# An identity load on another queue, a table spread and one product on GpSimd, and a new order of the work

## The chip, the cores and the metric

The kernel runs on one core of a Trainium2 chip. A core has TensorE (PE, matrix products into PSUM), VectorE (DVE), ScalarE (ACT), GpSimd (POOL) and SyncE (SP), which here only issues DMA transfers. Each engine works through its own list of instructions in order; semaphores tie the lists together. The metric is the time of one execution on the device, in microseconds (us). In the profile PEld are TensorE's weight loads, and SPq or ACTq is the issue of a transfer by SyncE or ScalarE.

## What is computed

The sequence length is 2048, the width 448 and the hidden width of the network 1792. A convolution mixer (a short shift filter, then a filter as long as the sequence) is followed by a network over the sequence positions; both have layer norms and residual sums.

```python
def _A_ref(q, k, v, shift_k, ssm_k, ssm_D):
    ...
    for t in range(ks):
        k_shift = k_shift + k_pad[:, t:t + S, :] * shift_k[:, ks - 1 - t][None, None, :]
    kv = k_shift * v
    ...
    y_f = kv_f * kf_f[None, :, :, :]
    y = irfft2(y_f)[:, 0, :S, :].astype(bfloat16)
    y = y + kv * ssm_D[None, None, :]
    return q * y

def _B_ref(x, w1, b1, w2, b2):
    h = _layernorm(x, axis=-1)
    u = jnp.einsum("bsd,sf->bdf", h, w1) + b1
    u = _gelu(u)
    y = jnp.einsum("bdf,fs->bds", u, w2) + b2
    return y.transpose(0, 2, 1)

h = x + _A_ref(_layernorm(x), A_k, A_v, A_shift_k, A_ssm_k, A_ssm_D)      # x = A_q
h2 = h + _B_ref(_layernorm(h), B_w1, B_b1, B_w2, B_b2)
```

## The kernel before

The 2048 positions lie as 128 partitions by 16 rows (r = 0 to 15). The long convolution is done as a Fourier transform in two stages by matmuls, a product, and the inverse in two stages.

The steps have short names, which the order uses:

- con: tables are loaded (L866). con.0 is the identity for the transposes, con.1 the first-stage table E0, con.2 the compact second-stage table FC. con.3 to con.6 spread FC into the table FW, one strided quarter each (L881 on ScalarE, L882 on VectorE), 128x1024 each; all four must be done before the second stage. con.7 to con.12 are tables of the inverse.
- loads: the inputs (L906 ssm_k, four blocks loads.1 to loads.4; L909 and L912 the shift weights, loads.5; L917 k, loads.6, 7, 9 and 11; L920 v; L924 ssm_D; L927 and L929 biases). xload (L934): q in four blocks of four rows, for the layer norm.
- kT: ssm_k is transposed by TensorE with the identity (L1083), eight transposes a step, and copied out of PSUM (L801 or L804). kT.0 and kT.1 are its first block, kT.2 and kT.3 the second, and so on.
- kv: k is transposed in the same way (L986), filtered by matmuls against diagonal weights (L1012, which L971 on GpSimd prepares) and multiplied by v on VectorE (L1051).
- k1 and u1: first transform stage of the filter and of kv, eight small matmuls a step (L1110; L1115 adds ssm_D), then a cast out of PSUM (L1126) on ScalarE or VectorE. Every second step a shuffle, a transfer from on-chip memory to itself (L1130), moves a quarter into the layout of the second stage. k1.0 to k1.7 are half as wide.
- k2 and u2: second stage, eight matmuls with FW (L1150) for two row pairs, and casts out of PSUM (L801/L802 on ScalarE, L804/L805 on VectorE).
- i1: the spectra are multiplied (L1176, 128x1792, VectorE, sixteen products), 64 small matmuls follow for each pair of products (L1195), two casts by ScalarE (L801) and two shuffles (L1210, L1215). zero is a memset on GpSimd (L1161).
- q and xn: statistics of the rows of q (L1252, L1254 on VectorE), then L1260 and the power -0.5 (L1263) on GpSimd, and the normalised rows 0 to 3 (L1285).
- i2: second inverse stage and what follows row by row: matmuls (L1316, L1321), a gate (L1330 on ScalarE, L1332 on VectorE), L1340 or L1351, statistics (L1357, L1360, L1369 and others), the power on GpSimd (L1396) and the normalised row (L1402).
- mlp: the network. Rows 0 to 15 for the first seven column blocks (L1449), the other seven blocks (L1459), the activation (L1439), the second matrix (L1470), the last sum (L1473), the output (L1478 to L1484).
- dummy and warm: matmuls whose result nobody reads (L1071, L1226).

The planner (_Sched) doesn't choose the order: the text ORDER lists for each engine every operation, as step:number, and so names the engine too. Its estimates and landing times (est, late, in nanoseconds) give each operation a modelled time, from which the slots of PSUM and of the small rings are assigned; the instructions and their waits are then written out. The first inverse stage is guarded by a mode: a product on VectorE and one on GpSimd aren't modelled as running together.

An engine goes through its list in order, so an operation that waits holds everything behind it on that engine, and a transfer that waits on SyncE holds the transfers behind it.

## Time and profile before

| | us |
|---|---|
| median of 3 runs | 171.25 |
| lowest, highest | 170.89, 171.83 |
| the profiled execution | 171.0 |
| its span in the profile | 169.2 |
| TensorE busy | 160.5 (95%), 1821 matmuls |
| VectorE busy | 94.5 (56%), 192 instructions |
| ScalarE busy | 88.1 (52%), 133 instructions |
| GpSimd busy | 17.4 (10%), 33 instructions |

The shares of the whole span hide that the stages differ: VectorE and ScalarE are full in the first 90 us and nearly idle afterwards. A busy TensorE isn't TensorE at its peak, since the ends of matmuls are modelled. The rows of the profile name a line of the kernel, an engine, an operation, the output and input with their shapes, the count, the busy time and the mean duration in ns; in a list in order of time the first two numbers are the start and the duration, and the bracket says how long the engine had been idle before, and what ended that. "Time to landing" of a transfer is from its issue to the arrival.

### The profile page before, as it was taken

What the parts mean: (1) busy time and instruction counts of PE and PEld (TensorE: products, weight loads), DVE (VectorE), ACT (ScalarE), POOL (GpSimd) and SP (SyncE); (2) the same over time, 40 slices, a digit from 0 to 9 for tenths busy, and PEclk for the clock granted to TensorE, in tenths of its full rate; (3) what the DMA queues carried; (4) which work ended last, traced back from release to release, by engine and by line L of the source; (5) the groups of instructions that cost most, each with busy time, mean ns of one, the idle gap of its engine ahead of it and who ended that gap; (6) DMA issues with size and microseconds to landing.
All of it is one profiled execution on the core that took longest, in us unless ns stands there. A gap on an engine that the chain in (4) does not pass through costs nothing.

```text
span 169.2 us, 4200 instructions
## 1 busy us (share of the span) xinstructions
PE 160.5 (95%) x1821; PEld 99.8 (59%) x1821; DVE 94.5 (56%) x192; ACT 88.1 (52%) x133; POOL 17.4 (10%) x33
## 2 busy tenths in 40 slices
PE   4999999999988988999999999999999999999994
PEld 1677777433333766644555555555567777777784
DVE  3149889999999999999987710000003223132232
ACT  3389998899999688899777508311210000000000
POOL 1013000000421000054253210000000000000000
PEclk9999999999999999999999999999999999999999
DMA  4999959689939344575899999990000111101111
GB/s 135 344 344 405 412 224 350 244 262 338 414 113 341 125 164 172 219 267 182 288 398 403 410 421 418 417 406 16 0 4 0 54 54 54 54 4 54 54 54 54
DMA packets 16416, 36.69 MB, mean 217 GB/s; under 512 B 2253, under 2 KB 9934, under 8 KB 16398
## 3 DMA queue, kind: packets, MB, share of 16 engines
q1 hardware_dynamic: 16254, 36.34, 57.7%
q8 instruction: 14, 0.23, 0.5%
q10 hardware_dynamic: 144, 0.08, 0.2%
q14 instruction: 4, 0.03, 0.0%
HBM read 23.69 MB, written 1.84 MB: 151 GB/s over the span
## 4 chain that ended last, share of the span: by engine, by line
PE 75%; ACT 14%; DVE 4%; DMA 3%; SPq 1%; issue 1%; POOL 1%
PE ps L1470 25%; PE ps L1449 13%; PE ps L1459 13%; PE ps L1110 6%; ACT arena L801 6%; PE ps L1012 4%; ACT arena L1126 4%; PE ps L1150 4%; PE ps L1195 3%; ACT arena L802 3%; DMA arena<-in_A_ssm_k_dram 3%; PE ps L986 2%; PE ps L1316 2%; DVE arena L1252 2%; PE ps L1083 2%; DVE arena L1176 1%
## 5 line engine op out<-in xcount | busy, mean ns | idle before, releaser
L1473 DVE SCALAR_TENSOR_TENSOR arena<-ps,arena 128x448 bf16<-128x448 f32 (+2 forms) x17 | 11.2, 657 | 57.5 <-PE ps L1470 57.5
L1470 PE MATMUL ps<-arena 128*128 128x448 bf16 (+2 forms) x238 | 42.7, 342 | 0.0
L1470 PEld LDWEIGHTS ps<-arena 128*128 128x128 bf16 x238 | 33.2, 144 | 9.5
L801 ACT CAST arena<-ps 128x896 bf16<-128x896 f32 (+1 forms) x28 | 23.2, 883 | 4.9 <-PE ps L1195 3.8
L1126 ACT CAST arena<-ps 128x896 bf16<-128x896 f32 (+2 forms) x28 | 21.5, 815 | 1.9 <-PE ps L1110 0.9
L1449 PE MATMUL ps<-arena 128*128 128x448 bf16 x112 | 22.4, 353 | 0.0
L1459 PE MATMUL ps<-arena 128*128 128x448 bf16 x112 | 21.4, 352 | 0.0
L1439 ACT ACTIVATE arena<-ps,arena 128x448 bf16<-128x448 f32 x14 | 8.2, 640 | 20.6 <-PE ps L1459 14.7
L1195 PE MATMUL ps<-arena 64*32 64x448 bf16 x512 | 16.1, 350 | 1.3 <-ACT arena L801 1.3
L1449 PEld LDWEIGHTS ps<-arena 128*128 128x128 bf16 x112 | 10.9, 98 | 10.6 <-ACT arena L1330 0.6
L1176 DVE TENSOR_TENSOR arena<-arena 128x1792 bf16<-128x1792 bf16 x16 | 17.0, 1086 | 0.0
L1459 PEld LDWEIGHTS ps<-arena 128*128 128x128 bf16 x112 | 11.0, 98 | 10.2 <-ACT arena L1439 0.2
L1110 PE MATMUL ps<-arena 128*32 128x448 bf16 (+2 forms) x288 | 16.6, 335 | 0.4
L1150 PE MATMUL ps<-arena 128*64 128x448 bf16 x128 | 14.7, 359 | 1.8 <-ACT arena L801 1.2
L1195 PEld LDWEIGHTS ps<-arena 64*32 64x32 f16 x512 | 11.6, 90 | 5.8 <-ACT arena L801 3.2
L1150 PEld LDWEIGHTS ps<-arena 128*64 128x64 f16 x128 | 5.6, 108 | 10.5 <-ACT arena L801 3.3
L1110 PEld LDWEIGHTS ps<-arena 128*32 128x32 f16 x288 | 7.3, 95 | 5.9 <-ACT arena L802 2.1
L804 DVE COPY arena<-ps 128x1024 bf16<-128x1024 bf16 (+1 forms) x9 | 5.7, 658 | 7.8 <-PE ps L1083 7.4
L1051 DVE TENSOR_TENSOR arena<-ps,arena 128x512 bf16<-128x512 f32 (+1 forms) x16 | 9.0, 617 | 1.0 <-PE ps L1012 0.9
L1252 DVE BATCH_NORM_STATS2 arena<-arena 128x6 f32<-128x448 bf16 x16 | 9.4, 607 | 0.0
L805 DVE TENSOR_SCALAR arena<-ps 128x896 bf16<-128x896 f32 x8 | 8.5, 1087 | 0.9 <-PE ps L1150 0.8
L1330 ACT ACTIVATE arena<-ps,arena 128x448 f32<-128x448 f32 x11 | 7.7, 719 | 2.3 <-PE ps L1316 2.2
(63 smaller groups left out, 152.0 us busy)
## 6 DMA issues: line engine op xcount, KB each, us to landing
arena<-arena SPq DMA_DIRECT2D x16, 448.0 KB, 5.0
arena<-in_B_w_dram SPq DMA_DIRECT2D x8, 896.0 KB, 11.5
arena<-in_B_w_dram SPq DMA_DIRECT2D x2, 2048.0 KB, 17.0
arena<-arena SPq DMA_DIRECT2D x15, 224.0 KB, 2.3
arena<-in_B_w_dram SPq DMA_DIRECT2D x2, 1536.0 KB, 18.8
arena<-in_A_k_dram SPq DMA_DIRECT2D x4, 448.0 KB, 6.1
arena<-in_A_v_dram SPq DMA_DIRECT2D x4, 448.0 KB, 7.9
arena<-in_A_q_dram SPq DMA_DIRECT2D x4, 448.0 KB, 6.1
```

The source lines that it names most:

```text
L801: return e.copy(out=dst(), in_=src())
L1051: return e.tensor_tensor(out=v, in0=u.rearrange("p t (r d) -> p t r d", d=64), in1=v, op=ALU.mult)
L1110: op("pe", lambda e, W, quad=quad, r=r, q=q, x=x, c0=c0, d0=d0, dw=dw: e.matmul(quad(x, q), E0[:, 128 * x + c0:128 * x + c0 + 32], src[:, ...
L1126: return e.copy(out=dst, in_=u) if W == "act" else e.tensor_copy(out=dst, in_=u)
L1150: op("pe", lambda e, W, b=bs[h], h=h, j=j, c=c, par=par: e.matmul(PS[64 * par:64 * par + 64, b.slots[c], 0:D], FW[:, 2 * j + h, 64 * c:64 ...
L1176: op("dve", lambda e, W, m=m, i=i: e.tensor_tensor(out=MR(m.slots[0]).rearrange("p (x y) d -> p x y d", x=2), in0=TU[:, i].unsqueeze(2).br ...
L1195: k = op("pe", lambda e, W, bs=bs, m=ms[h], par=par, t=t, tab=tab, xy=xy, g=g, qd=qd: e.matmul(PS[32 * qd:32 * qd + 32, bs[g >> 1].slots[g ...
L1252: op("dve", lambda e, W, bs=bs, r=r: e.bn_stats(out=bs, in_=X[:, r, :]), r=[(o_X + r * DB, DB)], w=[(ob, 24)], n=D, kind="1x")
L1449: op("pe", lambda e, W, r=r, fc=fc, b=bs[fc]: e.matmul(Pb(b), W1A[:, r, 128 * fc:128 * fc + 128], Q[:, r, :], start=(r == 0), stop=(r == R ...
L1459: op("pe", lambda e, W, r=r, fc=fc, b=b: e.matmul(Pb(b), W1B[:, r, 128 * (fc - n0):128 * (fc - n0) + 128], Q[:, r, :], start=(r == 0), sto ...
L1470: op("pe", lambda e, W, r=r, fc=fc, b=b, d0=d0, d1=d1: e.matmul(Pb(b)[:, d0:d1], W2[fc // 7][:, fc % 7, r:S:R], G[:, fc, d0:d1], start=(fc ...
L1473: op("dve", lambda e, W, r=r, b=b, d0=d0, d1=d1: e.scalar_tensor_tensor(out=X[:, r, d0:d1], in0=Pb(b)[:, d0:d1], scalar=bm[:, r:r + 1], in ...
```

## The change

The identity (con.0) is loaded by ScalarE, ahead of its table load, instead of third by SyncE. GpSimd may spread the table and may make products. In the new order it does two of the four spreads (con.5, con.6) and one of the sixteen products (i1.1); VectorE does con.4 and ScalarE con.3. The transposes begin with the first block of ssm_k, and SyncE's loads are ordered anew: first, third, fifth and seventh the ssm_k blocks 0, 1, 3 and 2, between them the small loads, then k, E0, more of k, the first rows of q, v, and FC. The planner takes a shuffle to land 700 or 350 ns later instead of 360 or 0, and an issue by ScalarE to cost 700 instead of 1400. Every engine's list is rearranged; beside what is named here, some casts change between ScalarE and VectorE (as many of the first and second stage in the one direction as in the other), and some small operations change engine.

```diff
-            o.est = {e: (585.0 if e == "pool" else 1400.0 if e == "act" else 700.0 if keng <= 8 else 460.0) for e in o.engs}
+            o.est = {e: (585.0 if e == "pool" else 700.0 if e == "act" else 700.0 if keng <= 8 else 460.0) for e in o.engs}
...
-            def cload(o, src, n, dt=f16):
-                op("sp", lambda e, W: e.dma_start(view(o, [n], dt), src), w=[(o, 2 * n)], dmab=128 * 2 * n)
+            def cload(o, src, n, dt=f16, W="sp", est=None):
+                op(W, lambda e, W: e.dma_start(view(o, [n], dt), src), w=[(o, 2 * n)], dmab=128 * 2 * n, est=est)
             sch.t0 = -60.0
-            cload(o_ID, d_id, 192, bf16)
+            cload(o_ID, d_id, 192, bf16, "act", 600.0)
...
-                op(FX, spread, r=[(o_FC, 2064)], w=[(o_FW, 8192, "fw")], n=1024, est={"act": 1150.0, "dve": 450.0})
+                op(("act", "dve", "pool"), spread, r=[(o_FC, 2064)], w=[(o_FW, 8192, "fw")], n=1024,
+                   est={"act": 1150.0, "dve": 450.0, "pool": 2850.0})
...
-                       dmab=128 * 4 * DB, keng=16, rate=300.0, late=360.0 if i >= 2 else 0.0))
+                       dmab=128 * 4 * DB, keng=16, rate=300.0, late=700.0 if i >= 2 else 350.0))
...
-                    op("dve", lambda e, W, m=m, i=i: e.tensor_tensor(
+                    op(("dve", "pool"), lambda e, W, m=m, i=i: e.tensor_tensor(
...
-                       r=[ru, (o_TK + i * 2 * DB, 2 * DB)], bw=[m], n=4 * D, after=aft, mode=1)
+                       r=[ru, (o_TK + i * 2 * DB, 2 * DB)], bw=[m], n=4 * D, after=aft, mode=1, est={"dve": 1005.0, "pool": 3450.0})
```

Of the order, the new lists that the prediction speaks of (TensorE's from the first transposes to the second stage, VectorE's to the first network rows, GpSimd's, SyncE's first part):

```diff
 "pe":
+        "dummy.0:2-10 kT.0:0-7 kT.1:0-7 kT.1:9 kT.3:0-7 kT.2:0-7 kT.3:9 kT.7:0-7 kT.6:0-7 kT.5:0-7 kT.4:0-7 kT.5:9 "
+        "kv.3:0-7 k1.12:0-7 k1.0:0-9 k1.8:0-7 k1.16:0-7 kv.7:0-7 kv.5:0-7 k1.13:0-7 k1.14:0-7 k1.9:0-7 k1.1:0-9 "
+        "kv.1:0-7 kv.8:0-3 kv.6:0-11 kv.8:4-11 k1.10:0-7 k1.11:0-7 kv.13:0-27 kv.15:0-27 kv.14:0-23 kv.2:0-3 "
+        "kv.4:0-11 kv.2:4-11 kv.9:0-27 k1.17:0-7 k1.18:0-7 kv.10:0-23 k1.19:0-7 k1.15:0-7 k1.2:0-9 k1.4:0-9 u1.8:0-7 "
+        "k1.6:0-9 k1.3:0-9 k1.5:0-9 kv.12:0-23 kv.11:0-27 k1.7:0-9 u1.9:0-7 u1.10:0-7 u1.0:0-7 u1.1:0-7 kv.16:0-23 "
+        "u1.2:0-7 k2.5:0-3 k2.4:0-3 u1.12:0-7 k2.9:0-3 k2.8:0-3 u1.13:0-7 u1.4:0-7 u1.14:0-7 u1.5:0-7 k2.15:0-3 "
...
 "dve":
+        "u1.5:8 k2.15:5 u1.3:8 u1.11:8 k2.3:4 q.1:4 q.2:1 k2.11:4 k2.13:5 k2.1:4 u2.9:5 k2.7:4 u2.13:4 u2.1:5 i1.0:0 "
+        "u2.11:4 q.3:2 q.3:0 u2.15:5 q.4:0 i1.13:0 i1.14:0 i1.7:0 i1.8:0 i1.9:0 i1.10:0 i1.12:0 i1.11:0 q.3:3 i1.5:0 "
+        "i1.6:0 i1.3:0 i1.2:0 i1.15:0 q.4:2 q.5:2 xn.0:1 i1.16:0 q.4:1 q.3:1 q.6:0 q.5:0-1 xn.2:0 q.5:3 q.6:1 q.4:3 "
...
 "pool":
+        "kv.0:1-2 loads.14:0 q.0:1 kv.0:0 kv.0:3 q.0:0 con.5:0 con.6:0 q.1:5 xn.0:0 q.2:4-5 i1.1:0 zero.0:0 q.4:4 "
+        "xn.3:0 q.6:4-5 q.4:5 i2.7:0 i2.15:0 i2.27:0 i2.40:0 i2.53:0 q.8:5 i2.66:0 i2.79:0 i2.92:0 i2.105:0 i2.0:0 "
...
 "sp":
+        "loads.1:0 loads.5:2 loads.2:0 loads.14:1 loads.4:0 loads.5:1 loads.3:0 loads.5:0 loads.7:0 con.1:0 "
+        "loads.11:0 loads.9:0 loads.15:0-1 loads.6:0 xload.0:0 loads.12:0 loads.13:0 loads.8:0 con.2:0 k1.9:9 "
+        "k1.11:9 k1.13:9 loads.10:0 k1.17:9 k1.19:9 k1.3:11 k1.15:9 k1.7:11 u1.9:9 con.7:0 u1.1:9 u1.13:9 u1.5:9 "
```

2 lines of the change are left out of this document (removed), and 81 rows, old and new, of the table ORDER.

## The prediction

> **What bounds the kernel now.** I read the busy time by stage first, then the chain that ended last, then the order of time on each engine. Columns of the first view: stretch, its length, busy time and count of TensorE, weight loads, VectorE, ScalarE and GpSimd, clock, share and rate of DMA.
>
> ```profile
> core 0: us, PE busy (x) PEld busy (x) DVE busy (x) ACT busy (x) POOL busy (x), PEclk, DMA share, GB/s
> 12.00:31.90 19.90, 19.90 (x484) 14.77 (x473) 18.02 (x32) 18.25 (x25) 2.10 (x2) 1.00 0.85 322
> 31.90:50.02 18.12, 16.43 (x196) 5.96 (x194) 17.26 (x22) 17.38 (x21) 2.30 (x6) 1.00 0.86 305
> 50.02:54.30 4.28, 3.77 (x34) 1.46 (x30) 4.28 (x6) 4.16 (x6) 1.42 (x2) 1.00 0.82 274
> 54.30:72.30 18.00, 16.72 (x518) 11.82 (x516) 17.99 (x28) 13.78 (x17) 0.00 (x0) 1.00 0.47 176
> 79.47:92.40 12.93, 12.93 (x69) 6.52 (x68) 11.15 (x46) 10.09 (x27) 5.13 (x7) 1.00 1.00 364
> ```
> ```profile
> 58.77 0.43 PE ps L1195 x8
> 59.20 1.71 ACT arena L801 x2
> 103.19 21.19 PE ps L1459 x112
> 124.37 42.51 PE ps L1470 x238
> ```
>
> Four stages with four limits. Until 31.9 us TensorE has no gap. From there to 54.3 it loses 18.12 - 16.43 = 1.69 and 4.28 - 3.77 = 0.51, together 2.2 us, while VectorE and ScalarE, which empty PSUM, are nearly full: this stage is bound by the evacuations. From 54.3 to 72.3 (first inverse stage) VectorE, which makes the products, is full, and the chain alternates between TensorE and ScalarE. From 79.47 TensorE is full, and it stays so in the chain down to the last row. So the last 90 us are fixed work, and a gain exists only if the row-wise network starts earlier than at 79.47 us. None of the edits touches a matmul of it.
>
> **The change part by part.** The altered estimates and landing times are numbers of the planner; they issue nothing. What runs differently is the engine or place of operations.
>
> *The front.* These are the loads that let the transposes begin; the last two rows are the time to landing of the ssm_k loads and of the k loads.
>
> ```profile
> 0.72 0.39 SPq L906 DMA_DIRECT2D arena<-in_A_ssm_k_dram  x1
> 1.80 0.57 SPq L866 DMA_DIRECT2D arena<-c_id  x1
> 2.42 1.53 SPq L906 DMA_DIRECT2D arena<-in_A_ssm_k_dram  x3
> 3.99 0.58 SPq L917 DMA_DIRECT2D arena<-in_A_k_dram  x1
> 5.54 1.29 PEld L1083 LDWEIGHTS ps<-arena 128*128 128x128 bf16 x16 [0.35 <-DMA arena<-c_id]
> 7.17 1.21 PE L1083 MATMUL ps<-arena 128*128 128x128 bf16 x16 [0.21 <-DMA arena<-in_A_ssm_k_dram]
> 8.32 0.42 SPq L866 DMA_DIRECT2D arena<-c_fw  x1
> 10.77 0.61 PE L986 MATMUL ps<-arena 128*128 128x128 bf16 x8
> DMA to landing us min/median/max: 3.6/5.1/5.6
> arena<-in_A_k_dram SPq DMA_DIRECT2D x4, 448.0 KB, 6.1
> ```
>
> The first transposes wait for the identity (5.54), the second block for the second ssm_k load (7.17). Issued by ScalarE at the start, the identity no longer holds 2.42 - 1.80 = 0.62 us of SyncE's queue, and the second ssm_k load goes out at 1.80 instead of 2.42. That can move 7.17 by up to 0.62. ScalarE pays one issue of about 0.57 ahead of its table load; its first evacuation comes after 6 us, and that idle time covers it. Against this stands the next need, the first block of k: in the new order two small loads and the long load of the shift weights come before it, so it is issued at about 4.9 instead of 3.99 (five issues of about half a us from 2.3 on), and 6.1 later is 11.0, where the transposes of k would be due at 10.77 - 0.6. So most of the 0.62 is lost again: I take -0.2, ends -0.6 and +0.5. [...]
>
> *The evacuation stage.* Prices:
>
> ```profile
> L881 ACT ACTIVATE arena<-arena 128x1024 f16<-128x1024 f16 x3 | 3.5, 1163 | 0.0
> L882 DVE TENSOR_SCALAR arena<-arena 128x1024 f16<-128x1024 f16 x1 | 0.5, 477 | 0.0
> L801 ACT COPY arena<-ps 128x1024 bf16<-128x1024 bf16 x6 | 5.9, 1019 | 4.6 <-PE ps L1083 4.6
> L1126 ACT CAST arena<-ps 128x512 bf16<-128x512 f32 x3 | 1.8, 587 | 0.8 <-PE ps L1115 0.8
> L1252 DVE BATCH_NORM_STATS2 arena<-arena 128x6 f32<-128x448 bf16 x12 | 7.0, 608 | 0.0
> L971 POOL TENSOR_TENSOR arena<-arena 128x1024 bf16<-128x1024 bf16 x1 | 1.9, 1906 | 0.1
> ```
>
> Counting the two orders, token by token, after the transposes of ssm_k and up to the first product: ScalarE gives up two of its three spreads (-2 x 1.16 = -2.33), takes one copy of transposed k more (+1.02) and one half-width cast less (-0.59): -1.9. VectorE gives one spread to GpSimd and takes one from ScalarE (0 net at 0.48), exchanges a copy for a half cast (about 0), and does four statistics instead of six before the first product (-2 x 0.61 = -1.2). All other casts are exchanged one for one. GpSimd's two spreads are not in the trace: bounds are 0.48 each (VectorE's form) and 1.9 (GpSimd's two-input form of the same size; it may run a little over); I take 1.9, so they end some 4 us after the table lands. The table is issued last but a few at about 11 us instead of 8.32, lands, by the 6.1 of the k loads, near 17, and the second stage needs it after 31 (31.68, L1150, below): 10 us of cover, and without it each late us would be one us of the end.
>
> What the relief is worth: the spreads lie before 31.9, where TensorE has no gap, so their 2.33 buys little. In the next stage the 2.2 us of gaps is the most that can be won. The 1.2 of statistics shared by two engines is 0.6; all relief shared, (1.9 + 1.2)/2, is 1.55. I take -0.9; ends 0 and -2.2.
>
> *The first inverse stage.* One product moves to GpSimd; the statistics taken out above are put behind the first product.
>
> ```profile
> 50.02 1.07 DVE L1176 TENSOR_TENSOR arena<-arena 128x1792 bf16<-128x1792 bf16 x1
> 54.11 7.27 DVE L1176 TENSOR_TENSOR arena<-arena 128x1792 bf16<-128x1792 bf16 x7
> 68.92 1.07 DVE L1176 TENSOR_TENSOR arena<-arena 128x1792 bf16<-128x1792 bf16 x1
> 57.00 1.71 ACT L801 CAST arena<-ps 128x896 bf16<-128x896 f32 x2 [0.92 <-PE ps L1195]
> 72.31 0.91 ACT L801 CAST arena<-ps 128x896 bf16<-128x896 f32 x1 [0.47 <-PE ps L1226]
> 12.38 1.09 DVE L1126 CAST arena<-ps 128x896 bf16<-128x896 f32 x1 [0.27 <-PE ps L1110]
> ```
>
> By elements the product on GpSimd takes 1906 x 1792/1024 = 3.34 us (VectorE: 7.27/7 = 1.04); ends 2.9 and 4.4, since overhead and pattern are unknown. It starts when the first product has ended, 1.0 after that product's start S, so it is ready at S + 4.5; before, the same operand was ready at 54.11 + 1.04 = 55.15, S + 5.1. Meanwhile VectorE has, by its order, two casts (1.09 each) and three statistics (0.61 each): 4.0 us from S + 1.0, so the next product starts at S + 5.0, behind GpSimd's end. Then 14 products of 1.03, two statistics and crumbs of 0.2: the last ends at S + 5.0 + 14.4 + 1.2 + 0.2 = S + 20.8; before, 69.99 - 50.02 = S + 20.0. The stage itself runs on a loop of PSUM pairs: evacuations at 57.00 and 72.31, seven steps of 2.19, above two products (2.06), so VectorE's chain has slack against it. Before, the first pair's last product ended at 55.15 and was evacuated from 57.00, 1.85 later; the same 1.85 behind S + 20.8 is S + 22.65, and before it was 72.31 - 50.02 = S + 22.3. So +0.3; ends 0 (the loop sets the end) and +1.4 (product of 4.4).
>
> [...]
>
> *The way to the network.* One normalisation goes from ScalarE to VectorE, and ScalarE evacuates the last two pairs without one between.
>
> ```profile
> 74.56 2.07 ACT L1285 ACTIVATE arena<-arena 128x448 f32<-128x448 bf16 x3
> 74.61 0.68 DVE L1351 SCALAR_TENSOR_TENSOR arena<-ps,arena 128x448 bf16<-128x448 f32 x1 [0.25 <-PE ps L1321]
> ```
>
> ScalarE is freed by 2.07/3 = 0.7 of the three it does behind the last cast. Behind the last product VectorE had seven statistics until 74.61, and will have four and a normalisation (about 1.4 less), but it waits 0.25 for TensorE there already, so only some 0.3 of it counts. Two deferred statistics (1.2) and a gate come between the first rows' normalisations instead, part of it in VectorE's free 12.93 - 11.15 = 1.8 us. I take -0.3; ends -0.8 and +0.6.
>
> **Sum:** -0.2 - 0.9 + 0.3 - 0.3 = -1.1 us on the profiled execution of 171.0 (span 169.2), so 169.9; the median shown is 171.25, and the forecast is 171.25 - 1.1 = 170.15.
>
> **Rivals.** *The second stage waits for a shuffle (slower).* The shuffle of the last even quarter (k1.3:11) has to land before the second stage's first matmul.
>
> ```profile
> 23.11 0.34 PE L1110 MATMUL ps<-arena 128*32 128x192 bf16 x7
> 27.94 1.73 PE L1012 MATMUL ps<-arena 64*128 64x256 bf16 x52
> 31.19 0.56 PE L1110 MATMUL ps<-arena 128*32 128x448 bf16 x8
> 31.68 0.95 PE L1150 MATMUL ps<-arena 128*64 128x448 bf16 x8
> arena<-arena SPq DMA_DIRECT2D x8, 448.0 KB, 4.6
> DMA to landing us min/median/max: 2.8/5.0/7.8
> ```
>
> Before, TensorE had 31.68 - 23.45 = 8.2 us of other work between them. In the new order it has two half groups (0.34 each), 52 + 24 convolution matmuls (1.73 + 0.8) and five full groups (5 x 0.56): 6.0. Cast and queue take about 0.5, so a landing of 5.5 us is hidden, and each us over it stalls TensorE, with the evacuations behind it. The eight of 22 to 34 us have a median of 4.6, which speaks against it; the slowest of all took 7.8, and the new order sends this one closer behind others. From 6.6 on the whole gain is gone; at 7.8 the stall is 2.3, and the time 170.15 + 2.3 = 172.4.
>
> *The relief is hidden anyway (no change).* If TensorE's matmuls, not the casts, set 31.9 to 54.3 as they do before it, the term of 0.9 falls away and with it the earlier S: -0.2 + 0.3 - 0.3 = -0.2, 171.05. For it: the gapless 19.90. Against: 2.2 us of gaps.
>
> *All of it counts (more gain).* -0.6 at the front, -1.55 in the evacuations, 0 in the inverse stage, -0.3: -2.45, 168.8. Against: it needs the k load to come in time although it is issued later.
>
> *The change does not do what it says:* the identity comes earlier but the first ssm_k block is later, so nothing starts earlier; that is the front term at 0, inside the forecast (170.35).
>
> **How the numbers follow.** Forecast 0.42 (own range 169.3 to 171.0), shuffle stall 0.27, hidden 0.16, all counts 0.15. Range: 168.8 to 172.4 holds all four but the tails of the outer two. What can be told from no change begins at 0.5%, 0.86 us: faster is below 170.4, slower above 172.1. Faster: two thirds of 0.42 and all of 0.15, 0.43. Slower: 0.21 of the 0.27 (the stalls above 2 us), and 0.04 from the hidden case with a late k load or a slow product on GpSimd (their upper ends, +0.5 and +1.4), 0.25. Same: the rest, 0.32.
>
> **What would show it.** Right: transposes from about 4.5 us; the second ssm_k block near 6.6; the first product at about 49; GpSimd's product of 3.3 to 3.5 us ending before VectorE's second; first network matmul at about 78.4; the rest unchanged at 90 us. Wrong: a wait of L1150 on a shuffle, of L986 on a k load, of a product on GpSimd, or of a statistic on the rows of q; or the network beginning at 79.5 or later.

## The result, and the profile after

| | before | after |
|---|---|---|
| median of the runs beside each other, us | 171.28 (22 runs, 170.71 to 172.65) | 172.12 (22 runs, 171.33 to 173.13) |
| profiled execution, us | 171.0 | 173.13 |
| its span, us | 169.2 | 171.3 |

The changed kernel is slower: after over before is 1.0044, interval 1.0024 to 1.0064, about 0.75 us (the medians differ by 0.84). The profiled execution of after is the slowest of its 22 runs, so its trace shows the losses larger than the median has them. A second profile of the same kernel, at 172.27 us, is the first experiment below.

The busy time by stage, after, cut at the same events as the prediction's rows (columns as there). The last row is the first inverse stage.

```profile
33.02:50.44 17.42, 15.76 (x180) 5.21 (x176) 16.33 (x20) 15.90 (x20) 1.86 (x4) 1.00 0.76 261
54.67:73.80 19.13, 16.57 (x518) 12.02 (x516) 18.35 (x29) 14.31 (x19) 2.10 (x3) 1.00 0.63 228
```

The evacuations were relieved: from 33.02 on ScalarE is busy for 15.90 of 17.42 us, where it had 17.38 of 18.12. TensorE's gaps did not close: 17.42 - 15.76 = 1.66 us, where there had been 1.69. And the first inverse stage has 19.13 - 16.57 = 2.6 us without a matmul, before 18.00 - 16.72 = 1.3.

The order of time in after, on TensorE, VectorE and GpSimd (start, duration, instruction; the bracket is the idle time before and what ended it):

```profile
4.71 1.38 PE L1083 MATMUL ps<-arena 128*128 128x128 bf16 x16
9.27 1.20 PE L1083 MATMUL ps<-arena 128*128 128x128 bf16 x16 [0.21 <-DMA arena<-in_A_ssm_k_dram]
10.70 0.62 PE L986 MATMUL ps<-arena 128*128 128x128 bf16 x8
33.02 0.95 PE L1150 MATMUL ps<-arena 128*64 128x448 bf16 x8
50.44 1.09 DVE L1176 TENSOR_TENSOR arena<-arena 128x1792 bf16<-128x1792 bf16 x1 [0.28 <-DMA arena<-arena]
51.61 3.59 POOL L1176 TENSOR_TENSOR arena<-arena 128x1792 bf16<-128x1792 bf16 x1 [6.64 <-DVE arena L1176]
55.07 7.09 DVE L1176 TENSOR_TENSOR arena<-arena 128x1792 bf16<-128x1792 bf16 x7
62.21 2.20 PE L1195 MATMUL ps<-arena 64*32 64x448 bf16 x74 [1.49 <-issue]
75.99 0.55 PE L1316 MATMUL ps<-arena 128*128 128x448 bf16 x2 [1.17 <-DMA arena<-arena]
81.30 0.92 PE L1449 MATMUL ps<-arena 128*128 128x448 bf16 x4
```

Four things stand here. The transposes begin 1.1 us earlier (4.71, before 5.78), yet those of k at 10.70 against 10.77: the fourth block of ssm_k is waited for at 9.27. The first product begins at 50.44 and not at 50.02, released by a transfer from on-chip memory to itself, a shuffle. GpSimd's product does what was said of it. And in the middle of a group of L1195 TensorE stands still for 1.49 us, released by nothing that the profile shows ("issue").

ScalarE's casts measure what that gap costs, since they follow each other at a fixed step. After:

```profile
57.38 1.71 ACT L800 CAST arena<-ps 128x896 bf16<-128x896 f32 x2 [0.95 <-PE ps L1195]
59.57 1.71 ACT L800 CAST arena<-ps 128x896 bf16<-128x896 f32 x2 [0.47 <-PE ps L1195]
62.87 1.71 ACT L800 CAST arena<-ps 128x896 bf16<-128x896 f32 x2 [1.58 <-PE ps L1195]
73.80 1.72 ACT L800 CAST arena<-ps 128x896 bf16<-128x896 f32 x2 [0.40 <-PE ps L1226]
```

The step is 2.19 (57.38 to 59.57), as before; the one over the gap is 3.30, so the gap costs 1.11. The network starts at 81.30 instead of 79.47, 1.83 later, and this adds up: first product +0.42; from there to the first of these casts 57.38 - 50.44 against 57.00 - 50.02, -0.04; the casts up to the last pair 73.80 - 57.38 against 72.31 - 57.00, +1.11; the rest up to the network 81.30 - 73.80 against 79.47 - 72.31, +0.34. Behind it stand 171.3 - 81.30 = 90.0 us, before 169.2 - 79.47 = 89.7, so another 0.27 was lost there.

SyncE's queue stands around both places. Its issues in order of time, first before, then after:

```profile
34.02 2.05 SPq L866 DMA_DIRECT2D arena<-c_et  x2
39.75 0.60 SPq L866 DMA_DIRECT2D arena<-c_et  x1
42.14 3.01 SPq L1130 DMA_DIRECT2D arena<-arena  x3
49.66 0.39 SPq L1422 DMA_DIRECT2D arena<-in_B_w_dram  x1
50.10 0.97 SPq L934 DMA_DIRECT2D arena<-in_A_q_dram  x2
51.12 0.67 SPq L866 DMA_DIRECT2D arena<-c_ew  x1
```
```profile
43.22 2.00 SPq L1130 DMA_DIRECT2D arena<-arena  x3
45.26 1.43 SPq L934 DMA_DIRECT2D arena<-in_A_q_dram  x1
46.73 1.20 SPq L865 DMA_DIRECT2D arena<-c_et  x1
50.44 0.38 SPq L1422 DMA_DIRECT2D arena<-in_B_w_dram  x1
50.86 0.97 SPq L865 DMA_DIRECT2D arena<-c_et  x2
51.88 0.52 SPq L934 DMA_DIRECT2D arena<-in_A_q_dram  x1
52.44 0.47 SPq L865 DMA_DIRECT2D arena<-c_et  x1
52.96 0.48 SPq L865 DMA_DIRECT2D arena<-c_ew  x1
53.48 0.47 SPq L934 DMA_DIRECT2D arena<-in_A_q_dram  x1
```

The network's first weight load (w1a.0, L1422) goes out at the moment the last u1 shuffle has landed, in both kernels (49.66 and 50.44; that transfer ends a wait of 1.8 and 1.0 us of SyncE); whatever stands behind it waits with it. Before, three of the tables c_et had gone out by 40.35, and behind w1a.0 stood two q blocks and one table. After, three tables c_et more stand behind it, so that six transfers follow it from 50.86 to 53.95. The rates of all transfers (last column) then differ, first before, then after:

```profile
56.00:58.00 2.00, 2.00 (x70) 1.71 (x61) 2.00 (x3) 1.08 (x3) 0.00 (x0) 1.00 0.18 60
58.00:60.00 2.00, 1.84 (x69) 1.27 (x61) 2.00 (x3) 1.53 (x3) 0.00 (x0) 1.00 0.02 7
```
```profile
56.00:58.00 2.00, 2.00 (x75) 1.91 (x61) 2.00 (x3) 1.05 (x2) 0.73 (x1) 1.00 0.97 358
58.00:60.00 2.00, 1.78 (x65) 1.22 (x61) 2.00 (x3) 1.53 (x3) 0.00 (x0) 1.00 0.91 355
```

One more queue moves its packets over these DMA engines: "q8 instruction", with 14 packets, together 0.23 MB, in the profile of either kernel. Asked in slices of a quarter of a us, the packet of this stage stands at 56.25 to 56.50 before, and at 60.00 to 60.25 after (packets, MB, share of 16 engines):

```profile
q8 instruction: 1, 0.02, 25.7%
```
```profile
q8 instruction: 1, 0.02, 23.1%
```

In both it comes just as the burst of loads ends, and after it TensorE goes on 2.2 us later, at 62.21. The theory that the experiments were to test: **a block of TensorE's instructions arrives too late, because the tables that were moved behind the weight load are still being transferred.** For the later first product the theory was SyncE's order of the last three u1 shuffles: the cast of u1.15 on ScalarE ends at 43.20, and as its shuffle was put ahead of those of u1.11 and u1.7, all three go out in one run from 43.22.

### The profile page after: what moved, and what is told of

It reads as the page before. It is cut to its first block, busy times and chain, and to the rows that moved or that the text cites. A ratio compares the mean times of both kernels' runs of the same rounds, so it can differ in the third digit from the quotient of the medians.

```text
span 171.3 us, 4206 instructions
## 1 busy us (share of the span) xinstructions
PE 161.3 (94%) x1821; PEld 100.0 (58%) x1821; DVE 95.9 (56%) x196; ACT 83.8 (49%) x127; POOL 26.9 (16%) x35
## 4 chain that ended last, share of the span: by engine, by line
PE 78%; ACT 12%; DMA 5%; SPq 2%; issue 2%; DVE 0%
PE ps L1470 25%; PE ps L1459 12%; PE ps L1449 12%; ACT arena L800 7%; PE ps L1110 7%; PE ps L1150 5%; PE ps L1012 4%; PE ps L1195 4%; PE ps L1316 4%; ACT arena L801 3%; DMA arena<-in_A_ssm_k_dram 3%; PE ps L986 3%; DMA arena<-arena 2%; ACT arena L1126 1%; SPq L906 1%
## 5 line engine op out<-in xcount | busy, mean ns | idle before, releaser
L1449 PE MATMUL ps<-arena 128*128 128x448 bf16 x112 | 22.5, 352 | 0.0
L1126 ACT CAST arena<-ps 128x896 bf16<-128x896 f32 (+2 forms) x27 | 21.0, 827 | 3.0 <-PE ps L1110 2.8
L1459 PE MATMUL ps<-arena 128*128 128x448 bf16 x112 | 21.4, 352 | 0.0
L1195 PE MATMUL ps<-arena 64*32 64x448 bf16 x512 | 15.8, 350 | 2.6 <-issue 1.5
L1150 PE MATMUL ps<-arena 128*64 128x448 bf16 x128 | 14.9, 360 | 1.7 <-ACT arena L801 0.7
L1176 DVE TENSOR_TENSOR arena<-arena 128x1792 bf16<-128x1792 bf16 x15 | 15.8, 1085 | 1.0 <-PE ps L1195 0.7
L1195 PEld LDWEIGHTS ps<-arena 64*32 64x32 f16 x512 | 11.8, 90 | 6.7 <-ACT arena L800 2.7
L1150 PEld LDWEIGHTS ps<-arena 128*64 128x64 f16 x128 | 5.3, 108 | 11.0 <-ACT arena L801 3.2
L803 DVE COPY arena<-ps 128x1024 bf16<-128x1024 bf16 x9 | 6.0, 689 | 7.7 <-PE ps L1083 5.6
L1369 ACT ACTIVATE arena<-arena 128x448 bf16<-128x448 bf16 x14 | 8.1, 575 | 3.8 <-DVE arena L1340 2.1
L1316 PE MATMUL ps<-arena 128*128 128x448 bf16 x32 | 8.5, 353 | 1.2 <-DMA arena<-arena 1.2
```

The costliest lines, as they stand in the source:

```text
L1126: return e.copy(out=dst, in_=u) if W == "act" else e.tensor_copy(out=dst, in_=u)
L1150: op("pe", lambda e, W, b=bs[h], h=h, j=j, c=c, par=par: e.matmul(PS[64 * par:64 * par + 64, b.slots[c], 0:D], FW[:, 2 * j + h, 64 * c:64 ...
L1176: op(("dve", "pool"), lambda e, W, m=m, i=i: e.tensor_tensor(out=MR(m.slots[0]).rearrange("p (x y) d -> p x y d", x=2), in0=TU[:, i].unsqu ...
L1195: k = op("pe", lambda e, W, bs=bs, m=ms[h], par=par, t=t, tab=tab, xy=xy, g=g, qd=qd: e.matmul(PS[32 * qd:32 * qd + 32, bs[g >> 1].slots[g ...
L1316: k = op("pe", lambda e, W, b=b, r=r, h=h: e.matmul(Pb(b), ET[:, 2 * r + h, :], TZ[:, h, slot[r], :], start=(h == 0), stop=(h == 1 and r > ...
L1449: op("pe", lambda e, W, r=r, fc=fc, b=bs[fc]: e.matmul(Pb(b), W1A[:, r, 128 * fc:128 * fc + 128], Q[:, r, :], start=(r == 0), stop=(r == R ...
```

## The experiments

All times are in us. A ratio is to the kernel before, run beside it on the same chip; the medians of before were 171.39, 171.32 and 171.46 in the three sets (1 to 4, 5 to 8, 9 to 11). S is the start of the first product; the first regular cast is the first of ScalarE's casts that follow each other at the fixed step (57.00 before, 57.38 after).

**1. The changed kernel again** (no edit).

> The changed kernel once more, for a second trace. Fetch theory (the gap of 1.49 us inside the first inverse stage is TensorE waiting for its next block of instructions, which stands behind the w1, table and q loads that are issued at 50.4 to 53.5 us): the gap is there again at about 60.7 us, between 0.7 and 2 us long, and the first network matmul comes between 80.5 and 81.5. Rival, an accident of the one profiled execution: no gap over 0.3 us in that stage, and the network begins at about 80.0 us. Both expect the last shuffle of the u1 steps to land at about 50.4.

172.27 us. From this profile, TensorE and ScalarE:

```profile
61.78 2.20 PE L1195 MATMUL ps<-arena 64*32 64x448 bf16 x74 [0.87 <-issue]
59.77 1.71 ACT L800 CAST arena<-ps 128x896 bf16<-128x896 f32 x2 [0.47 <-PE ps L1195]
62.44 1.71 ACT L800 CAST arena<-ps 128x896 bf16<-128x896 f32 x2 [0.96 <-PE ps L1195]
```

The gap is there again, at the same matmul, and smaller: the packet of instructions stands at 59.25. The step over it is 2.67, a loss of 0.48. S is 50.65 (+0.63) and the network starts at 80.45 (+0.98), with another 0.26 behind it. So in this profile some 0.6 is lost ahead of the first product and 0.5 in the gap; the medians differ by 0.84.

**2. The shuffle of u1.15 last of the three.**

```diff
 "sp":
-        "u1.3:9 u1.15:9 u1.11:9 u1.7:9 "
+        "u1.3:9 u1.11:9 u1.7:9 u1.15:9 "
```

> The changed kernel with the shuffle of u1.15 issued behind those of u1.11 and u1.7 instead of ahead of them. Queue theory (u1.15 is cast last, and its wait holds two finished shuffles, so that three go out within 1.3 us at 43.2 to 44.4 and the last takes 6.0 us to land): two shuffles go out before 43, the last at about 43.3 lands at 48.5 to 49.3, the second stage no longer waits 0.67 us for it, and the first product starts at about 49.2 instead of 50.44; the kernel is 0.5 to 1.2 us faster than the changed one. Rival (the casts, not the landing, hold the first product): the first product moves by less than 0.3 us and the time stays within 0.3 us of the changed one.

171.19 (170.74 to 172.43, 12 runs), ratio 0.9986, interval 0.9958 to 1.0014, against 1.0044 (1.0024 to 1.0064) without the edit. SyncE, and TensorE:

```profile
41.62 2.09 SPq L1130 DMA_DIRECT2D arena<-arena  x3
49.28 0.38 SPq L1422 DMA_DIRECT2D arena<-in_B_w_dram  x1
```
```profile
61.12 2.20 PE L1195 MATMUL ps<-arena 64*32 64x448 bf16 x74 [0.59 <-issue]
63.54 1.53 PE L1195 MATMUL ps<-arena 64*32 64x448 bf16 x53 [0.22 <-ACT arena L800]
65.81 2.23 PE L1195 MATMUL ps<-arena 64*32 64x448 bf16 x75 [0.73 <-issue]
```

The run of shuffles starts 1.6 earlier and has landed at 49.28 instead of 50.44; S is 49.89, 0.55 earlier. One token of the order gives back what the change lost. Little of that comes through the first product: the first regular cast is at 57.19, against 57.38 in after and 57.58 in experiment 1, and 0.18 of this lies in the transposes of k (10.52 against 10.70), which the edit doesn't touch. What else it moves is the weight load behind the shuffles, and with it the burst of tables. In this profiled execution, of 172.09, there are still gaps.

**3. The tables early**, without the edit before.

```diff
 "sp":
-        "u1.9:9 con.7:0 u1.1:9 u1.13:9 u1.5:9 u1.3:9 u1.15:9 u1.11:9 u1.7:9 xload.1:0 con.9:0 w1a.0:0 con.10:0 con.11:0 xload.3:0 con.12:0 con.8:0 xload.2:0 "
...
-        "w1a.1:0 w1a.2:0 "
+        "u1.9:9 con.7:0 con.9:0 con.11:0 u1.1:9 u1.13:9 u1.5:9 xload.1:0 con.10:0 u1.3:9 u1.15:9 u1.11:9 u1.7:9 w1a.0:0 xload.3:0 con.8:0 xload.2:0 "
...
+        "w1a.1:0 con.12:0 w1a.2:0 "
```

> The changed kernel with three inverse tables and the second q block issued where the kernel before has them, ahead of the last u1 shuffles, instead of behind the w1 load. Fetch theory: transfers are over by about 57 us, the instruction block comes before 59, the gap of 1.49 us is gone, and the last two pairs are cast 1.1 us earlier relative to the first; the time is 0.5 to 1.2 us below the changed kernel, unless the shuffles behind the tables land later by as much (their landing is read separately). [...]

171.83 (171.38 to 172.47, 12 runs), ratio 1.0011 (0.9983 to 1.0039). The packet of instructions stands at 57.50, no gap is left, and the first six pairs of casts follow at 2.19. But S is 50.90, and the first regular cast is at 57.87, against 57.38 and 57.58 in the changed kernel: with the tables ahead of them the last shuffles land later (the weight load, which waits for them, goes out at 50.89 instead of 50.44). The interval overlaps that of the changed kernel (1.0024 to 1.0064), so a gain in time isn't shown.

**4. The kernel before, its identity loaded by ScalarE** and nothing else changed.

```diff
 "act":
-        "dummy.0:1 "
+        "con.0:0 dummy.0:1 "
 "sp":
-        "loads.2:0 loads.5:2 con.0:0 loads.1:0 "
+        "loads.2:0 loads.5:2 loads.1:0 "
...
-            cload(o_ID, d_id, 192, bf16)
+            cload(o_ID, d_id, 192, bf16, "act", 600.0)
```

> The kernel before with the identity alone moved to ScalarE's queue; nothing else is changed. Theory (the identity gives 0.6 to 0.8 us at the front, and the new order of the loads gave it back by issuing the third ssm_k block at 4.05): first transposes at about 4.7, the block that started at 7.17 starts at about 6.6, the first transposes of k at 10.2 to 10.5 instead of 10.77, and the time is 0 to 0.6 us below the kernel before, less where the u1 shuffles set the first product. Rival (the transfers are full from 5.5 us on, so nothing after 8 us moves): k's transposes stay within 0.15 us of 10.77 and the time within 0.2 us.

171.18 (170.24 to 172.04, 12 runs), ratio 0.9975 (0.9948 to 1.0003). In its profile the transposes begin at 5.78, as before, and those of k at 11.32, which is 0.55 later: the expectation for the trace was missed, and a gain of 0.25% that the interval can't tell from none is all that the times show. The trace shows what held the transposes: nine dummy matmuls stand ahead of them on TensorE and begin at 2.44 (before 2.45), when VectorE has filled their operand.

**5. Both edits of SyncE's queue** (the last u1 shuffle, and the tables early).

> The changed kernel with both edits of SyncE's queue: the shuffle of u1.15 last, and the tables and the second q block ahead of the last u1 shuffles. Queue and fetch theory together: no gap over 0.3 us of TensorE inside the first inverse stage (as with the tables early), and the first product at 49.3 to 50.0 us instead of 50.9 (as with u1.15 last); the time is 170.5 to 171.1, under both single edits. Rival (the two edits cancel, since the tables go ahead of the shuffles on the same transfer engines and push their landing by what the other edit wins): the first product stays at 50.5 or later and the time at 171.5 or more.

171.44 (170.76 to 172.28, 12 runs), ratio 1.0008 (0.9989 to 1.0028). S is 50.27, there is no gap (packet at 57.00), and the first regular cast is at 57.39. The network starts at 79.22, 0.25 earlier than before, and the 0.27 behind it takes that back: with both losses gone the profiled span is that of the kernel before (169.2). Whether the two edits add up in time can't be told, since the interval overlaps that of the second experiment.

**6. The product back on VectorE.**

```diff
 "dve":
-        "u2.11:4 q.3:2 "
+        "u2.11:4 i1.1:0 q.3:2 "
 "pool":
-        "q.2:4-5 i1.1:0 zero.0:0 "
+        "q.2:4-5 zero.0:0 "
```

> The changed kernel with the one product back on VectorE, between the first cast behind the first product and the statistics. Theory (the product on GpSimd costs and gives next to nothing: 3.6 us, ended about when VectorE comes to its next product): the time stays within 0.4 us of the changed kernel, the gap of TensorE of 0.8 us or more at about 61 us is there again, VectorE's chain of products ends about 1 us later relative to the first. [...]

172.38 (171.78 to 172.53, 6 runs), ratio 1.0065 (1.0044 to 1.0086). The gap stays (0.40 us, packet at 59.25), the first regular cast comes later (58.13), and the time is, if anything, above the changed kernel's. The product on GpSimd is no cause of the loss.

**7. The two spreads back** on ScalarE (con.5) and VectorE (con.6).

```diff
 "act":
-        "con.3:0 kv.4:12 "
+        "con.3:0 kv.4:12 con.5:0 "
 "dve":
-        "con.4:0 q.2:0 "
+        "con.4:0 con.6:0 q.2:0 "
 "pool":
-        "q.0:0 con.5:0 con.6:0 q.1:5 "
+        "q.0:0 q.1:5 "
```

> The changed kernel with GpSimd's two spreads back, one on ScalarE and one on VectorE; GpSimd's took 5.7 us for both. Theory (the relief of the two engines lies where TensorE's matmuls and, after them, the landing of the shuffles set the pace): the first product moves by less than 0.3 us and the time stays within 0.4 us of the changed kernel. Rival (the relief counts, as the forecast had it): 0.5 us or more slower than the changed kernel, with a first product 0.5 us or more later.

172.08 (171.29 to 172.81, 12 runs), ratio 1.0054 (1.0034 to 1.0075). With 1.1 us more on ScalarE (36.18 busy from the transposes of k to the first product, after has 35.05) and 0.6 more on VectorE, second stage and first product stand where they stood, at 32.89 and 50.31, and no difference in time from the changed kernel is shown. But the transposes of k came 0.45 earlier in this profile (10.25), and that hides a loss: counted from them, the way to the end of the second stage takes 0.3 us longer (shown below, with the evacuations). So the relief is worth some 0.3 us of the trace, and not the 0.9 of the forecast.

**8. Both queue edits, and SyncE's first loads in the order of need.**

```diff
 "sp":
-        "loads.1:0 loads.5:2 loads.2:0 loads.14:1 loads.4:0 loads.5:1 loads.3:0 loads.5:0 loads.7:0 con.1:0 loads.11:0 "
+        "loads.1:0 loads.2:0 loads.4:0 loads.3:0 loads.7:0 con.1:0 loads.14:1 loads.5:2 loads.5:1 loads.11:0 loads.5:0 "
```

> Both queue edits, and SyncE's first loads with the four ssm_k blocks, the first k block and E0 ahead of the small loads, so that the block c2, issued at 4.05 in the changed kernel, goes out at about 2.1. Front theory (TensorE waits at 9.27 for that block, and this wait gives the identity's gain back): the wait is gone, k's first transposes come at 9.8 to 10.3 instead of 10.70, the second stage begins 0.4 to 0.8 us earlier, and the time is 0.3 to 0.8 us below the version with both queue edits alone. Rival (transfers are saturated from 5.5 us on, so the order only exchanges waits): k's first transposes within 0.2 us of 10.7, or the second stage within 0.2 us of where it was, and no difference in time.

170.96 (170.18 to 171.63, 12 runs), ratio 0.9979 (0.9961 to 0.9997). TensorE and VectorE:

```profile
9.48 0.61 PE L986 MATMUL ps<-arena 128*128 128x128 bf16 x8
49.67 1.09 DVE L1176 TENSOR_TENSOR arena<-arena 128x1792 bf16<-128x1792 bf16 x1 [0.75 <-DMA arena<-arena]
```

With the four blocks of ssm_k sent one after another the transposes of k begin 1.2 us earlier than in the run with both queue edits alone (10.68), and of this 0.6 reaches the first product, which again waits for the shuffles (0.75 us). How much of it comes in every execution is open: with the same first loads, experiments 10 and 11 have k's transposes at 10.68 and 10.27.

**9. The weight load behind the tables**, the only edit of the changed kernel.

```diff
 "sp":
-        "con.9:0 w1a.0:0 con.10:0 con.11:0 xload.3:0 con.12:0 con.8:0 xload.2:0 i1.1:68 "
+        "con.9:0 con.10:0 con.11:0 xload.3:0 con.12:0 con.8:0 xload.2:0 w1a.0:0 i1.1:68 "
```

> The changed kernel with one edit: the first weight load of the network (w1a.0) stands behind the tables con.10, con.11, con.12, con.8 and the q blocks xload.3 and xload.2 in SyncE's queue instead of ahead of them. In the changed kernel these wait with it for 50.44 us and then run together with the block of instructions. Theory (the instruction block is late behind those transfers): the tables go out at 45 to 48, the late block arrives before it is needed, the gap of 0.9 to 1.5 us between two groups of L1195 is gone, the network's first matmul at 80.0 to 80.5, time 171.0 to 171.5. Rival (the gap comes from the change's instructions themselves, wherever the loads stand): the gap stays, time 171.9 to 172.4. Third way: the tables wait for buffers of their own that come free only at about 50 us; then they go out where they did, nothing changes, and the weight load comes later.

171.29 (170.67 to 171.97, 12 runs), ratio 0.9993 (0.9971 to 1.0015), against 1.0044 (1.0024 to 1.0064) without the edit. The tables go out from 46.53 to 50.5, the weight load at 51.52. The packet stands at 58.50 and the gap is 0.39, not none as expected; the weight load now comes last in the burst. This gap cost nothing: the casts on both sides of it start at 59.37 and 61.57, the usual step. The network starts at 78.88, earlier than the 80.0 to 80.5 expected. Nothing but the place of loads in one queue was touched, so the loss in the gap belongs to them.

**10. The last u1 shuffle and the first loads**, the tables left behind the weight load.

```diff
 "sp":
-        "loads.1:0 loads.5:2 loads.2:0 loads.14:1 loads.4:0 loads.5:1 loads.3:0 loads.5:0 loads.7:0 con.1:0 loads.11:0 "
+        "loads.1:0 loads.2:0 loads.4:0 loads.3:0 loads.7:0 con.1:0 loads.14:1 loads.5:2 loads.5:1 loads.11:0 loads.5:0 "
...
-        "u1.3:9 u1.15:9 u1.11:9 u1.7:9 "
+        "u1.3:9 u1.11:9 u1.7:9 u1.15:9 "
```

> The changed kernel with the shuffle of u1.15 behind that of u1.7 (as in the second experiment, 171.19 us) and SyncE's first loads reordered (as in the eighth: the four blocks of ssm_k one after another, then k, the table E0 and the shift weights), the tables of the inverse left where the change put them. If the two add up, the transposes of k begin near 9.5 us, the first product at about 49.3, and the time is 170.5 to 170.8. If the late instruction block takes the gain back (the tables still stand behind the weight load), a gap of 0.6 to 1.5 us shows in L1195 and the time is 171.1 to 171.5.

170.88 (170.35 to 171.94, 12 runs), ratio 0.9976 (0.9954 to 0.9998). Between the two expectations in time, and without a gap: the packet stands at 58.25, just early enough. The transposes of k begin at 10.68 and not near 9.5, with waits of 0.28 and 0.35 for blocks of ssm_k, and S is 50.05 instead of 49.3. The transposes of k stand where the changed kernel has them (10.70), S is 0.39 earlier than there, and yet the first regular cast comes at 57.35 against 57.38: here too the earlier first product gained nothing.

**11. The same, with the weight load behind the tables:** the edit of 9 on top of 10.

```diff
 "sp":
-        "con.9:0 w1a.0:0 con.10:0 con.11:0 xload.3:0 con.12:0 con.8:0 xload.2:0 i1.1:68 "
+        "con.9:0 con.10:0 con.11:0 xload.3:0 con.12:0 con.8:0 xload.2:0 w1a.0:0 i1.1:68 "
```

> The kernel of the run before it, and w1a.0 behind the tables as two runs before. If the three effects (queue of the last u1 shuffle, first loads, tables ahead of the weight load) are separate: the first product at about 49.3, no gap in L1195, network's first matmul at 78.0 to 78.5, time 169.9 to 170.4, below every kernel so far. If the tables only trade the gap against a later landing of the last u1 shuffle (as the run with both queue edits suggests: first product 50.3 there), the first product is at 49.8 or later and the time 170.8 to 171.2, as with the tables early.

170.49 (170.27 to 171.42, 11 runs), ratio 0.9952 (0.9930 to 0.9973): below both kernels, with an interval that lies clear of 1. Its profiled execution took 170.43. SyncE; TensorE:

```profile
41.94 1.52 SPq L1130 DMA_DIRECT2D arena<-arena  x2
44.73 3.10 SPq L865 DMA_DIRECT2D arena<-c_et  x3
50.32 0.38 SPq L1422 DMA_DIRECT2D arena<-in_B_w_dram  x1
```
```profile
60.89 4.15 PE L1195 MATMUL ps<-arena 64*32 64x448 bf16 x128 [0.22 <-ACT arena L800]
78.62 1.11 PE L1449 MATMUL ps<-arena 128*128 128x448 bf16 x5
```

Shuffles first, then the tables in the time in which these land, then the weight load: S is 49.64, no gap, and the network starts at 78.62, 0.85 us earlier than in the kernel before. That is a little short of the first expectation (49.3, 78.0 to 78.5, 169.9 to 170.4) and nearer to it than to the second. The intervals of the three kernels below 1 (8, 10 and this one) overlap, so which of them is best isn't settled by them.

The packet can be set against the time at which it was due. The packets that come after it start at the earliest when TensorE has started 990, 1118 and 1246 matmuls, which is 128 apart (all three in experiment 8, the first two in experiment 3, the first before). So the one in question is due 128 matmuls ahead of the 990, at 862. That this is when it is asked for is inferred from these counts. The table has the start of the quarter-us slice of the packet; the start of the half-us slice at the end of the burst in which the transfers fell under 250 GB/s; how long after the start of the matmul behind the 862 the packet began; TensorE's idle time at the same place of the program, shown as "issue"; and by how much ScalarE's casts, from the first regular one to the last pair, exceed the 15.31 us of the kernel before.

| kernel | packet | transfers fall | late by | gap | cost |
|---|---|---|---|---|---|
| before | 56.25 | 56.0 | 0.24 | none | 0 |
| before, identity on ScalarE (4) | 57.25 | 57.0 | 0.42 | none | 0 |
| both queue edits (5) | 57.00 | 57.0 | 0.57 | none | 0 |
| tables early (3) | 57.50 | 57.5 | 0.70 | none | 0 |
| both queue edits and first loads (8) | 56.25 | 56.5 | 0.76 | none | 0 |
| last shuffle, first loads, weight load behind (11) | 57.00 | 57.0 | 1.03 | none | 0 |
| last shuffle, first loads (10) | 58.25 | 59.0 | 1.99 | none | 0 |
| weight load behind (9) | 58.50 | 58.5 | 2.21 | 0.39 | 0.01 |
| product on VectorE (6) | 59.25 | 59.5 | 2.22 | 0.40 | 0.01 |
| u1.15 last (2) | 58.75 | 58.5 | 2.52 | 0.59 | 0.56 |
| after again (1) | 59.25 | 60.0 | 2.67 | 0.87 | 0.48 |
| spreads back (7) | 59.00 | 59.5 | 2.80 | 0.83 | 0.46 |
| after | 60.00 | 59.5 | 3.52 | 1.49 | 1.11 |

Up to a lateness of 1.99 there is no gap, from 2.21 on always one, and on the whole it grows with the lateness. In all six with a gap TensorE goes on 2.2 to 2.6 us after the packet. The cost is some 0.4 less than the gap; 0.22 of that TensorE would have waited for ScalarE at the end of the group. Experiment 2 has a second gap (0.73 at 65.81), after its next packet, which came 2.1 us after the 990; its cost is that of both.

## Why the prediction was wrong

The forecast was 170.15 with a range of 168.8 to 172.4; the time was 172.12, inside the range and on the other side of before. Two of the four terms failed, the evacuations and the first inverse stage, and the 90 us behind the start of the network, which had been put at no change, grew by 0.27. The 2.1 us between the two profiled spans are made up so: transposes of k -0.07; from them to the first regular cast 46.68 instead of 46.23, +0.45; casts +1.11; way to the network +0.34; behind it +0.27. In the second profile of the changed kernel they are -0.06, +0.64, +0.48, -0.08 and +0.26.

**The front, -0.2.** Size about right: the transposes of k come at 10.70 against 10.77, and in the eight profiles with the change's first loads at 10.25 to 10.71. The reason was right only in part, so some of this is luck. The sum let the load of k come late, and it did by a little: the weight load for the first transposes of k had waited 0.34 us for it (six of the eight profiles have such a wait, 0.20 to 0.74). The sum left out the fourth block of ssm_k, which is issued seventh and was waited for as well (9.27, 0.21 idle). The first signs came as named: transposes at 4.71 (said: 4.5), the second block at 6.67 (said: 6.6). But the identity alone does not bring the first of them, as the fourth experiment shows: the nine dummy matmuls ahead of the transposes begin at 1.37 instead of 2.45, because the new list of VectorE fills their operand (dummy.0:0) ahead of its other first step (loads.0:0). Neither the prediction nor the description of the change names that swap. Whether another order of the first loads is worth more is open: the same first loads gave 9.48 in experiment 8 and 10.68 and 10.27 in 10 and 11.

**The evacuations, -0.9: the step that failed first.** The count was right. From the transposes of k to the first product, before and after:

```profile
10.77:50.02 39.25, 37.56 (x695) 21.61 (x695) 36.51 (x54) 36.57 (x47) 4.40 (x8) 1.00 0.86 315
```
```profile
10.70:50.44 39.74, 37.99 (x688) 20.95 (x688) 34.74 (x52) 35.05 (x44) 8.54 (x8) 1.00 0.82 296
```

VectorE lost 36.51 - 34.74 = 1.8 us of work and ScalarE 36.57 - 35.05 = 1.5, together 3.3 where 1.2 + 1.9 = 3.1 had been counted. TensorE's idle time is 39.25 - 37.56 = 1.69 before and 39.74 - 37.99 = 1.75 after. The step read "nearly full engines beside 2.2 us of gaps" as "the gaps are there because the engines are full". With the work taken off, they stay. And it gave the new order of the work no price of its own. The same work shows that price: from the transposes of k to the last 16 second-stage matmuls that don't need the last shuffle (47.44 before, 48.04 after) TensorE starts the same 672 matmuls, by line, in both kernels (the rows also count what runs over their edges). Before and after:

```profile
10.77:47.44 36.67, 35.52 (x675) 20.70 (x673) 33.93 (x51) 34.25 (x45) 4.07 (x7) 1.00 0.91 333
```
```profile
10.70:48.04 37.34, 36.24 (x673) 20.30 (x673) 32.62 (x50) 32.92 (x42) 8.54 (x8) 1.00 0.82 294
```

The stretch takes 37.34 us instead of 36.67, and since the idle time is 1.10 against 1.15, the rest counts as TensorE's busy time. In the ten profiles of the new order that have the spreads on GpSimd it takes 37.31 to 37.34, with the spreads back (experiment 7) 37.65. So the spreads' relief was worth 0.3, and the rest of the new order cost about 1.0. What in the order costs it, the runs don't show. Of the gaps that stay, those at the end of the stage are a loop: from 44.07 on TensorE does a group of eight matmuls in 0.99 us, ScalarE casts its result in 0.92, and in each step both stand idle for 0.23 to 0.27 until the other is done; the step is 1.98, before 1.97. The work taken off ScalarE elsewhere did not shorten this loop.

The first product waits for another event, the landing of the last shuffle. The kernel before had shown it, on GpSimd, in a row that the prediction left unread:

```profile
49.69 1.59 POOL L1161 MEMSET arena<- 128x1792 bf16 x1 [3.49 <-DMA arena<-arena]
```

The first product came at 50.02, a third of a us behind that landing. The shuffles are ended 0.8 later in after although SyncE is done issuing them at the same time (45.22 against 45.15): three go out in 2.0 us instead of 3.0, since the one that was held up stands first, and a q block and a table follow on their heels (45.26, 46.73). But the casts did not wait for it. Counted from the group at 47.44 or 48.04, the first product comes 2.58 us later before and 2.40 in after, the first regular cast 9.56 and 9.34 us later. In the three kernels with u1.15 last and the tables behind (2, 10, 11) the product comes after 2.05 us and the cast still after 9.34 or 9.35; where the product comes after 2.61 (experiment 1) the cast takes 9.55, and after 2.95 (experiment 3) 9.92. So in these profiles a landing costs what it comes later than some 2.4 us, which is nothing in after and 0.2 in its second profile. Putting that shuffle last took the ratio from 1.0044 to 0.9986, some 1.0 us, and the two intervals don't overlap; how much of this comes by the burst of loads, which goes out as soon as the last shuffle has landed, isn't separated.

**The first inverse stage, +0.3 (0 to +1.4): a term left out.** What the step costed was right. GpSimd's product took 3.59 us (said: 3.34), ended at 55.20 and VectorE's next product came at 55.07, S + 4.6 (said: S + 5.0), and with the product on VectorE nothing is gained. But the change also moves three tables of the inverse in SyncE's list to places behind the weight load: two from places before 40.35 us, one from behind the first inverse stage. No transfer of that list behind FC is in the sum. Each table is 256 KB:

```profile
arena<-c_et SPq DMA_DIRECT2D x3, 256.0 KB, 6.7
```

Three are 0.79 MB, an estimated 2.2 us at the 358 GB/s of this stage, and the burst ended 3.5 later (59.5 against 56.0); 0.8 of that is its later start (50.44 against 49.66), and 0.5 stays unexplained. None of these tables was waited for; the block of instructions that came only at the end of the burst was, as far as the table of the packets shows it. That is the +1.1 of the profiled execution and the +0.5 of the second one.

**The way to the network, -0.3.** +0.34 in the profile of after, with 1.17 us of waiting for a shuffle of the inverse stage (L1316 at 75.99); -0.08 and +0.07 in those of experiments 1 and 2, with 0.76 and 0.91 of such waiting. In the other eight profiles of the new order it is -0.60 to -0.78 (in the last experiment 78.62 - 72.24 = 6.38 against 79.47 - 72.31 = 7.16), also in 6 and 7, which have the late tables and the gap. So the mechanism was there, and a late shuffle covered it in three profiles; why it was late there isn't shown. Part of it is only moved: in all eleven profiles of the new order 90.0 us stand behind the network's first matmul, where the two of the old order have 89.7. TensorE has 477 matmuls from there on instead of 475, one more of L1316 and one of L1226, so the network's first matmul stands ahead of more of the inverse's work.

**The rivals.** The slower one, a shuffle that stalls the second stage, fell at its place (L1150 at 33.02 waits for none). Shuffles did land late, at the end of the second stage (0 to 0.2 us of cost) and on the way to the network. Its 172.4 is near the 172.12 for other reasons. "The relief is hidden anyway" was near the mark on the relief, of which 0.3 us came, but its 171.05 had no price for the new order nor for the instructions. Of the signs named for a wrong forecast two came, the network beginning at 79.5 or later and, in a small way, the wait on a k load; a gap released by nothing was not among them.

**What stays open.** What in the new order costs TensorE the 1.0 us up to the end of the second stage; why a shuffle of the inverse stage was late in three profiles; what the identity's queue alone is worth (0.9975, 0.9948 to 1.0003); and how much the order of the first loads gives from one execution to the next.

## What to carry to other kernels

A list of transfers is a queue with a head (here the weight load at 50.44, with six transfers behind it from 50.86 on): for every transfer that is moved, write down what it now stands behind, when that one can go, and what bursts out together when it does. Before an engine's relief is counted as time, find what ends each gap and what ends the stage, since two nearly full engines beside a gap are no proof that they make it: here the gaps were two engines taking turns, and the next stage's first instruction was not the one that the rest waited for. After the change, time the same work between the same two points of the program in every profile, and not against the clock, since a stage that starts earlier by chance hides what it lost. And keep bulk loads that nobody needs soon out of the us in which TensorE runs many small matmuls: here the packet of instructions came as such a burst ended, up to 3.52 us late by the count of matmuls, and TensorE stood still for up to 1.49 us.

## What the runs showed of the hardware

**TensorE stood still in the middle of its matmuls for 0.39 to 1.49 us, which the profile calls "issue".** A group of 64 matmuls of one instruction list was cut in the middle, at the same matmul give or take one in every profile that had the gap. In the second experiment's rows the cuts lie 74 + 53 = 127 matmuls apart, each with its weight load, and the earliest starts of the packets behind the one in question lie 128 matmuls apart (990, 1118, 1246). That it is this queue's packet that TensorE waits for is inferred from these counts and from the table, where on the whole the gap grows with the packet's lateness; no run moves the packet alone.

**The packet of instructions came as the burst of loads ended.** In all thirteen profiles of the table it comes within 0.75 us of the fall of the transfers' rate, between 56.0 and 60.0, and up to 3.52 us after it was due by the count of matmuls. The trace shows when the packet ran; when it was asked for is inferred, and why it ran no earlier isn't shown.

**GpSimd took 2.85 us for a one-input copy with a scale,** strided, 128x1024 f16. The prediction's bounds were 0.48 to 1.9, so the two-input row of the same size was no upper bound for it. It cost nothing, since the second stage began at 33.02, 7 us after the second spread had ended (26.07). The product of 128x1792, scaled by elements from that same two-input row, came within 8% (3.59 against 3.34).

```profile
L881 POOL TENSOR_SCALAR arena<-arena 128x1024 f16<-128x1024 f16 x2 | 5.7, 2849 | 8.7 <-DMA arena<-c_fw 8.7
```

The products of GpSimd (51.61 to 55.20) and VectorE (from 55.07) overlap by 0.13 us; what two such products cost each other when they run at the same time, these runs don't show.
